# The second group's preparation moved into the first group's recurrence, q turned by VectorE from the fourth group on, and one split moved earlier

## The chip, the core and the metric

The kernel runs on one core of a Trainium2 chip. The core has a matrix engine (TensorE, PE in the profile), three engines that work on vectors (VectorE = DVE, ScalarE = ACT, GpSimd = POOL) and a queue engine (SyncE = SP) that issues transfers. Each engine takes its instructions strictly in the order of its own list, and waits on semaphores where an operand comes from elsewhere. The metric is the time of one execution on the device in microseconds (us); of several runs the median counts.

## What is computed

Three layers follow one another on 3072 tokens of width 384: a delta-rule attention, a dense layer pair, and a layer with 8 experts.

```python
# attention: B=4, H=8, S=768, D=48; q, k, v [B,H,S,D], beta [B,H,S]
k_n = k / (np.linalg.norm(k, axis=-1, keepdims=True) + 1e-06)
for t in range(S):
    kt, vt, bt = (k_n[:, :, t], v[:, :, t], beta[:, :, t, None])
    y[:, :, t] = np.einsum('bhd,bhde->bhe', q[:, :, t], state)
    v_old = np.einsum('bhde,bhd->bhe', state, kt)
    state = state + bt[:, :, :, None] * np.einsum('bhd,bhe->bhde', kt, vt - v_old)
# dense pair: x [3072,384], w_in [384,2048], w_out [2048,384]
r = np.maximum(x @ w_in, 0.0)
x = (s * (r * r) + b) @ w_out
# experts: logits = normalised x times normalised embeddings / tau; one expert for each token
h = np.maximum(x[mask] @ w1[e], 0.0)
out[mask] = gate_w[mask, None] * (h @ w2[e])
```

## The kernel before, in words

**Attention.** The 768 positions are cut into 24 chunks of 32, and 4 chunks make a group: six groups, numbered 0 to 5 here (the "second group" is group 1). A group is first prepared, then run through the recurrence, chunk by chunk.

Preparation of a group: `load_k`, `load_n` (q), `load_beta`, `load_v` issue the transfers on SP; `tr_k` and `tr_q` turn k and q on PE (16 turns each, from `kpad` and `qpad` through PSUM tiles `pp`, copied by ACT into `kqt`); `gram` forms the products k k and k q on PE (tiles `gr`), ACT copies one half (`gc`), DVE masks the other (`mt`); `lanes_1` to `lanes_3` and `scale_v` bring norms and beta in on DVE; `solve` eliminates 31 columns one after another on DVE, two instructions each (`tmp`, `T`); `lanes_out` gives `tt`.

The recurrence step of a chunk (`dstep`) is a chain between PE and DVE: `ks` (PE, tile `ch`), `X` (DVE), `tx` (PE, tile `u`), `bdu` (DVE), `ku` (PE, tile `ds`) with the new state `sst` (DVE), and `mu` (PE, into `ch`), which ACT copies into `x`. In group 0 a few idle matmuls (`warm`) stand between. The chunk s of group g is written step (g,s) below: u(1,0) is the `u` of group 1's first step, ks(2,0) the `ks` of group 2's first.

**Dense pair.** `moe1` runs 12 tiles of 256 tokens, each with 8 pairs of `mm1` and `mm2`. Tile 0 uses the weights in float32 words that have to be put together first: 16 pieces are loaded (`w_load`, in the order `W_ORDER`), scaled by ACT (`w_scale`), and joined by `x_step` (two DVE instructions and one on POOL). From tile 1 on the weights are split in two parts (`split_step`, one ACT and one DVE instruction a piece) and the matmuls run in one pass each. Two groups' worth of tiles follow each group, so the attention runs ahead of the dense pair.

**Experts.** After the last tile `ffn1` and `ffn2` run over 6 supertiles of 512 tokens. Their inputs are split by `x2_split` (ACT, then POOL) in three pieces m = 0, 1, 2.

**What sets the order.** PE, DVE, ACT and POOL run in the order in which the program is written; SP's order is made by the scheduler. `attention` keeps a list of items with due times counted in hops (a step has three: `ks`, `u`, `ds`/`mu`; group 0's first step has two) and issues those due at each quarter hop. Between quarter hops `run_moe` issues a counted number of ticks of the dense pair. Items due at 100 or later are issued after the group's last step, each followed by `PREP` ticks. In group 0's recurrence the items are the `x_step`s, one a hop. Group 1's preparation stands at 99 and later, that is behind group 0's recurrence, among tile 0's matmuls. In the groups after that each group's preparation lies within the stage of the group before it.

All PSUM tiles named `pp`, `gr`, `u`, `ds`, `xp` share one pool of three buffers.

Of the kernel before, what the change touches and what calls it, by code (L numbers as in the profile page):

```python
# [6 lines left out]
F32 = mybir.dt.float32  # L7
# [12 lines left out]
def tile_kernel(ctx, tc, q, k, v, beta, w_in, w_out, s_in, b_in, emb, tau, w1, w2, out):  # L20
# [125 lines left out]
                    in_=beta[h, 2 * r:2 * r + 2, gi * HG * C:(gi + 1) * HG * C].rearrange("g (n t) -> g n t", t=C))  # L146

    def tr_k(gi, s, eng=None):
        kqt_t[gi, s] = att.tile([128, B, 256], F32, tag="kqt", name="kqt", bufs=KQB)[0:DP]
        pp = ps_pp.tile([128, B, 128], F32, tag="pp", name="pp")  # L150
        for h in range(B):
            nc.tensor.transpose(out=pp[0:DP, h, :], in_=kpad[gi % 2][:, h, s, 0:DP], identity=ident)
        o = kqt_t[gi, s].rearrange("p h (a x t) -> p (h a) x t", a=2, x=4)[:, :, 0::3, :]
        i = pp[0:DP].rearrange("p h (a x t) -> p (h a) x t", a=2, x=2)
        if eng is nc.vector:
            nc.vector.tensor_copy(out=o, in_=i)
        else:
            nc.scalar.copy(out=o, in_=i)
# [18 lines left out]

    def tr_q(gi, h):
        tr_n(gi, h, qpad, slice(1, 3), (nc.scalar,))

    def k_rows(gi, s):
        pp = ps_pp.tile([128, B, DP], F32, tag="pp", name="kr")
# [112 lines left out]
            tt_t[gi] = att.tile([128, 2 * HG * B, C], F32, tag="tt", name="tt", bufs=2)  # L295
        nc.vector.transpose(out=tt_t[gi].rearrange("p u t -> p t u"), in_=T)

    PREP = {100: 2, 200: 5, 201: 4, 300: 2, 301: 1, 400: 5}
    st = {"hop": 0, "xs": 0, "pos": -1, "xd": {}, "gi": 0, "left": 0}

    def ks(gi, s, ch):
# [112 lines left out]
    def attention(more, first):  # L414
        for gi in range(NG):
# [4 lines left out]

            if gi == 0:
                add(0, first)
                for i in range(1, 3 * HG - 1):
                    add(i, x_step)
                add(10, x_step)
            if gi + 1 < NG:
                g2 = gi + 1
                sy = [nc.sync]
                if gi:
                    add(0, load_k, g2, sy)  # L430
                    add(0, load_n, g2, qpad, q, nc.sync)
                    add(0, load_beta, g2)
                    add(0, load_v, g2, nc.sync)
                h = 3.25
                if gi:
                    for f in (tr_k, tr_q, gram):
                        for s in range(0, HG, 2 if f is gram else 1):
                            add(h, f, g2, s)
                            h += 0.25
                else:  # L440
                    add(99, second_places)
                    for f in (tr_k, tr_q, gram):
                        for s in range(0, HG, 2 if f is gram else 1):
                            add(99 if f is tr_k and s < 2 else 100, f, 1, s)
                if gi:
                    for f, a in ((lanes_1, ()), (lanes_2, ()), (lanes_3, ()), (scale_v, (0, nc.vector)),
                                 (scale_v, (1, nc.vector))):
                        add(h, f, g2, *a)
                        h += 0.25
                    he = 11.25  # L450
                    for j in range(C - 1):
                        add(h + (he - h) * j / (C - 1), solve, g2, j)
                    add(he + 0.25, lanes_out, g2)
                else:
                    add(100, router_setup_a2)
                    add(200, lanes_1, 1)
                    add(200, lanes_2, 1)
                    add(200, lanes_3, 1)
                    add(201, scale_v, 1, 0, nc.vector)
                    add(201, scale_v, 1, 1, nc.vector)  # L460
                    add(201, router_setup_b)
                    for j in range(C - 1):
                        add(301 if j % 3 == 2 else 300, solve, 1, j)
                    add(400, lanes_out, 1)
            items.sort(key=lambda x: (min(x[0], 300) if x[0] > 100 else x[0], x[1]))

# [333 lines left out]
    with tc.manual_schedule(engines={ET.PE, ET.DVE, ET.Activation, ET.Pool}):  # L800
# [15 lines left out]
            w_load(W_ORDER[i])  # L816
        nc.sync.dma_start(out=s_sb, in_=s_in.partition_broadcast(128))
        nc.sync.dma_start(out=b_sb, in_=b_in.partition_broadcast(128))
        for i in W_ORDER[4:8]:
            w_load(i)  # L820
        for i in W_ORDER[8:]:
            w_load(i)
        router_setup_a()
        load_k(1, sy)
        gc_tile(0)
        ga = ps_a.tile([128, 2, HG * B, C], F32, tag="acc", name="gr")
        for h in range(B):
# [18 lines left out]
            tr_q(0, h)  # L846
        load_n(1, qpad, q, nc.sync)
        load_beta(1)
        load_v(1, nc.sync)
        for s in range(HG):  # L850
            k_rows(0, s)
        w_scale(11)
        for s in range(HG):
            gram_first(1, s, cg)
        for j in range(C - 1):
            solve(0, j)
            if j == 26:
                tg = ln[0][1]
                nc.tensor.matmul(out=warm_t[0][0:32, 0, 0:32], lhsT=tg[:, 25, 0:32], rhs=tg[:, 26, 0:32],
                                 start=True, stop=True)  # L860
                warm(9)
# [12 lines left out]
        def run_moe(n):  # L874
            for _ in range(n):
# [4 lines left out]
                    state["m"] = False  # L880
                    return
                state["n"] += 1
                if state["n"] % 3 == 0:
                    if cv["n"] < NU:
                        x_step()
                    elif state["n"] >= 76:
                        split_step()

        at = attention(lambda: run_moe(1), masks)
        for ticks in at:  # L890
# [264 lines left out]
        for s_ in range(NST):  # L1155
            if s_ + 2 < NST:
                x2_load(s_ + 2)
            for t in range(NTS):
# [1 line left out]
                    ffn1(s_ + 1, 2 * t)  # L1160
                    ffn1(s_ + 1, 2 * t + 1)
                ffn2(s_, t)
                if s_ + 2 < NST and t:
                    x2_split(s_ + 2, t - 1)
                if (s_, t) == (0, 0):
                    router2b()
                for _ in range(2):
# [54 lines left out]
```

## Time and profile before

| | us |
|---|---|
| runs | 917.24, 921.82, 922.56 |
| median | 921.82 |
| profiled execution, time | 918.63 |
| its span in the trace | 916.8 |
| PE busy | 839.4 (92%) |
| PE weight load busy | 770.5 (84%) |
| DVE busy | 465.3 (51%) |
| ACT busy | 458.4 (50%) |
| POOL busy | 61.9 (7%) |
| mean granted PE clock | 0.948 |

The span is the time from the first to the last instruction in the trace; the 1.8 us beyond it belong to the run's start and end. PE's busy time is modelled: its matmuls are pipelined, and a busy PE need not run at its peak. The page's chain of work that ended last holds only the last output tile, so it tells nothing of the stages that the change touches; these are read from the timeline and from windows.

### The profile page before, as it was taken

Reading aid. Unit: us, or ns where it says so; the run is one execution under the profiler, and the core shown is the slowest. Engines: PE = TensorE matmul, PEld = TensorE weight load, DVE = VectorE, ACT = ScalarE, POOL = GpSimd, SP = SyncE. Lnnn points to the kernel's source line nnn. Section 1 sums busy time; section 2 is a strip of 40 time slices with the busy share of each in tenths; the row PEclk is TensorE's granted clock in tenths of the full one; section 3 lists DMA queues with packets and bytes.
Section 4 is the critical chain, followed back from the end, with each engine's and each line's share of the span. In section 5 each row is a group of like instructions: output and inputs, shape, how many; then the busy total and the mean of one; then the engine's idle time right before and its main releaser. Section 6 shows DMA issues by size and latency. Waiting matters only on the chain. (4 is left out here: it accounts for less than half of the span.)

```text
span 916.8 us, 27694 instructions
## 1 busy us (share of the span) xinstructions
PE 839.4 (92%) x12090; PEld 770.5 (84%) x12090; DVE 465.3 (51%) x1051; ACT 458.4 (50%) x861; POOL 61.9 (7%) x71
## 2 busy tenths in 40 slices
PE   6467797876999999999999999999999999999996
PEld 4345686775989999999999999999997889889895
DVE  2979588669537942795368632225215423321101
ACT  1544646733575567565756566678653222222211
POOL 5115400000000000000000000000001011011000
PEclk7557899877999999999999999999999999999999
DMA  8683114211220222022000000015002910132000
GB/s 162 195 310 65 28 26 75 48 23 25 47 57 4 47 44 54 3 41 49 20 4 20 3 19 2 19 34 157 19 1 53 56 61 18 60 122 102 26 26 27
DMA packets 115593, 49.42 MB, mean 54 GB/s; under 512 B 89943, under 2 KB 112144, under 8 KB 115472
## 3 DMA queue, kind: packets, MB, share of 16 engines
q1 hardware_dynamic: 108560, 46.44, 22.4%
q10 hardware_dynamic: 6336, 1.18, 0.9%
q8 instruction: 95, 1.56, 0.7%
q14 instruction: 26, 0.21, 0.1%
q0 software_dynamic: 576, 0.02, 0.1%
HBM read 38.06 MB, written 9.74 MB: 52 GB/s over the span
## 5 line engine op out<-in xcount | busy, mean ns | idle before, releaser
L672 PE MATMUL acc<-gh,wp 128*128 128x256 f32 x1056 | 145.4, 284 | 0.0
L672 PEld LDWEIGHTS acc<-gh,wp 128*128 128x128 f32 x1056 | 132.6, 192 | 1.4
L635 ACT ACTIVATE r<-h 128x512 f32<-128x512 f32 x96 | 57.7, 601 | 130.5 <-PE h L627 103.4
L627 PE MATMUL h<-xh,wp 128*128 128x256 f32 x576 | 118.7, 289 | 2.4 <-ACT r L635 1.2
L627 PE MATMUL h<-xhl,wp 128*128 128x256 f32 x720 | 102.2, 287 | 0.0
L627 PEld LDWEIGHTS h<-xh,wp 128*128 128x128 f32 x576 | 94.5, 191 | 3.7 <-ACT r L635 1.6
L920 DVE SCALAR_TENSOR_TENSOR hl<-h,hh 128x512 fp32r<-128x512 f32 x46 | 31.8, 690 | 121.0 <-ACT hh L919 121.0
L649 DVE TENSOR_TENSOR gl<-r,gh 128x512 fp32r<-128x512 f32 x88 | 60.3, 685 | 62.4 <-ACT gh L647 62.4
L627 PEld LDWEIGHTS h<-xhl,wp 128*128 128x128 f32 x720 | 90.4, 189 | 1.1
L627 PE MATMUL h<-xl,wp 128*128 128x256 f32 x288 | 81.0, 281 | 0.0
L672 PE MATMUL acc<-gl,wp 128*128 128x256 f32 x528 | 76.3, 280 | 1.1 <-issue 1.1
L646 ACT ACTIVATE r<-r,b_sb,s_sb 128x512 f32<-128x512 f32 x88 | 72.0, 818 | 2.2
L377 ACT COPY x<-ch 32x384 f32<-32x384 f32 x96 | 45.2, 471 | 48.6 <-PE ch L363 47.5
L672 PEld LDWEIGHTS acc<-gl,wp 128*128 128x128 f32 x528 | 67.8, 190 | 1.3 <-issue 1.2
L289 DVE TENSOR_TENSOR T<-T,tmp 128x31 f32<-128x31 f32 (+15 forms) x186 | 65.1, 350 | 6.4
L993 POOL TENSOR_TENSOR x2l<-xr,x2h 128x512 fp32r<-128x512 f32 x15 | 19.4, 1291 | 719.4 <-DVE L L1090 592.7
L286 DVE TENSOR_TENSOR tmp<-A,T 128x31 f32<-128x31 f32 (+15 forms) x186 | 64.6, 348 | 5.0
L1003 PE MATMUL o<-w2h,hh 128*128 128x384 f32 x184 | 62.6, 340 | 0.0
L636 ACT ACTIVATE r<-r 128x512 f32<-128x512 f32 x96 | 60.7, 632 | 3.1
L1003 PE MATMUL o<-w2h,hl 128*128 128x384 f32 x184 | 62.2, 338 | 0.0
L1003 PE MATMUL o<-w2l,hh 128*128 128x384 f32 x184 | 62.1, 337 | 0.0
L1007 ACT ACTIVATE o<-o,gate 128x384 f32<-128x384 f32 x24 | 14.0, 582 | 94.1 <-PE o L1003 85.3
(215 smaller groups left out, 1437.9 us busy)
## 6 DMA issues: line engine op xcount, KB each, us to landing
wr<-in_moe_w_in SPq DMA_DIRECT2D x16, 384.0 KB
wr<-in_moe_w_out SPq DMA_DIRECT2D x8, 768.0 KB
v<-in_v SPq DMA_DIRECT2D x192, 24.0 KB
x2d<-x2s SPq DMA_DIRECT2D x24, 192.0 KB
out<-o SPq DMA_DIRECT2D x24, 192.0 KB
kpad<-in_k SPq DMA_DIRECT2D x160, 24.0 KB
qpad<-in_q SPq DMA_DIRECT2D x40, 96.0 KB
xr<-x2d SPq DMA_DIRECT2D x5, 768.0 KB
```

The lines of the kernel that those rows point to most:

```text
L286: nc.vector.tensor_tensor(out=tmp, in0=A[:, j + 1:, j:j + 1].to_broadcast([128, m, j + 1]), in1=T[:, j:j + 1, 0:j + 1].to_broadcast([128, ...
L289: nc.vector.tensor_tensor(out=T[:, j + 1:, 0:j + 1], in0=T[:, j + 1:, 0:j + 1], in1=tmp, op=ALU.subtract)
L377: nc.scalar.copy(out=x_t[gi][pb:pb + C, :, r * 96:(r + 1) * 96].rearrange("p h (g e) -> p h g e", g=2), in_=y[32 * rr:32 * rr + 32, :, :, ...
L627: nc.tensor.matmul(out=h[:, f, :], lhsT=wi_(w, 2 * j + f, m), rhs=x[:, m, :], start=(m == 0 and i == 0), stop=(m == KD - 1 and i == 2))
L635: nc.scalar.activation(out=r, in_=h, func=AF.Relu)
L636: nc.scalar.activation(out=r, in_=r, func=AF.Square)
L646: nc.scalar.activation(out=r, in_=r, func=AF.Identity, scale=s_sb, bias=b_sb)
L649: later.append((step[0] + 11, lambda: nc.vector.tensor_tensor(out=gl, in0=r, in1=gh.bitcast(F32), op=ALU.subtract)))
L672: nc.tensor.matmul(out=acc[:, m * TT:(m + 1) * TT], lhsT=wo_(w, 2 * j + f, m * 128, 128) if kk else wx_(2 * j + 1, 2 * j + f, m * 128), rh ...
L920: nc.vector.scalar_tensor_tensor(out=hl, in0=ps, scalar=0.0, in1=hh.bitcast(F32), op0=ALU.max, op1=ALU.subtract)
L993: nc.gpsimd.tensor_tensor(out=xl[:, m].rearrange("p (u t) -> p u t", u=NTS), in0=xr[:, :, m, :], in1=o.bitcast(F32), op=ALU.subtract)
L1003: nc.tensor.matmul(out=ps, lhsT=h[:, sl], rhs=w[:, f, :], start=(f == 0 and i == 0), stop=(f == KF2 - 1 and i == 2))
```

## The change

Four things are changed. (1) Group 1's k is loaded right after the first four weight pieces, its q and beta after eight, its v after twelve; its `tr_k` for chunks 0 to 2 is issued before the `warm` matmuls that stand ahead of group 0's first step, and the rest of its turns, its `gram`, its `lanes` and the first eight `solve` columns are due inside group 0's recurrence (hops 2 to 10.5). (2) Of the `x_step`s six instead of twelve lie in that recurrence; the others follow one every 8 ticks of tile 0, and the remaining `solve` columns of group 1, `scale_v` and the router's setup are spread among them, three ticks each. (3) For groups 3, 4 and 5 q is no longer turned on PE: `load_qb` loads it in 64 pieces a group instead of 8, laid out in 32 by 32 blocks, and `tr_qb` turns it by four DVE transposes a head straight into `kqt`; only three heads fit, so the fourth head's 16 pieces wait until the first head has been turned. (4) In the experts' layer the third `x2_split` piece is issued with the second, one ffn2 earlier.

```diff
@@ tr_k @@
-        kqt_t[gi, s] = att.tile([128, B, 256], F32, tag="kqt", name="kqt", bufs=KQB)[0:DP]
+        kqf_t[s] = att.tile([128, B, 256], F32, tag="kqt", name="kqt", bufs=KQB)
+        kqt_t[gi, s] = kqf_t[s][0:DP]
...
+    qn = qpad.rearrange("p h r d -> p (h r d)")[:, 0:3 * HG * 128].rearrange(
+        "p (h s r d) -> p h s r d", h=3, s=HG, r=4)
...
+    def load_qb(gi, h):
+        for g in range(2):
+            for b in range(2):
+                w = min(32, D - 32 * b)
+                for s in range(HG):
+                    t = (gi * HG + s) * C
+                    nc.sync.dma_start(
+                        out=qn[32 * (2 * g + b):32 * (2 * g + b) + 32, h % 3, s, :, 0:w],
+                        in_=q[h, g::2, t:t + C, 32 * b:32 * b + w].rearrange("r t d -> t r d"))
+
+    def tr_qb(gi, h):
+        for s in range(HG):
+            o = kqf_t[s][:, h].rearrange("p (a x t) -> p a x t", a=2, x=4)[:, :, 1:3, :]
+            nc.vector.transpose(out=o, in_=qn[:, h % 3, s].rearrange("p (a x) d -> p a x d", a=2))
...
-    PREP = {100: 2, 200: 5, 201: 4, 300: 2, 301: 1, 400: 5}
+    PREP = {300: 3, 400: 5}
@@ attention, group 0 @@
-                for i in range(1, 3 * HG - 1):
+                for i in range(1, 7):
                     add(i, x_step)
-                add(10, x_step)
@@ attention, a later group @@
-                    add(0, load_n, g2, qpad, q, nc.sync)
+                    if g2 < 3:
+                        add(0, load_n, g2, qpad, q, nc.sync)
+                    else:
+                        for x in range(3):
+                            add(0, load_qb, g2, x)
+                        add(4.25, load_qb, g2, 3)
...
-                    for f in (tr_k, tr_q, gram):
+                    if g2 > 2:
+                        h = 2.75
+                    for f in (tr_k, tr_qb if g2 > 2 else tr_q, gram):
                         for s in range(0, HG, 2 if f is gram else 1):
+                            if f is tr_qb and s == 3:
+                                h = 5
                             add(h, f, g2, s)
                             h += 0.25
@@ attention, group 1's preparation @@
-                    for f in (tr_k, tr_q, gram):
-                        for s in range(0, HG, 2 if f is gram else 1):
-                            add(99 if f is tr_k and s < 2 else 100, f, 1, s)
+                    add(2, tr_k, 1, HG - 1)
+                    for s in range(HG):
+                        add(2.5 + 0.5 * s, tr_q, 1, s)
+                    add(5, gram, 1, 0)
+                    add(5.75, gram, 1, 2)
...
-                    add(200, lanes_1, 1)
-                    add(200, lanes_2, 1)
-                    add(200, lanes_3, 1)
+                    add(7, lanes_1, 1)
+                    add(7.75, lanes_2, 1)
+                    add(8.25, lanes_3, 1)
                     for j in range(C - 1):
-                        add(301 if j % 3 == 2 else 300, solve, 1, j)
+                        if j < 8:
+                            add(8.75 + j * 0.25, solve, 1, j)
+                        else:
+                            add(300, solve, 1, j)
...
@@ start of the program @@
+        load_k(1, sy)
         for i in W_ORDER[4:8]:
             w_load(i)
-        for i in W_ORDER[8:]:
-            w_load(i)
-        router_setup_a()
-        load_k(1, sy)
...
         load_n(1, qpad, q, nc.sync)
         load_beta(1)
+        for i in W_ORDER[8:12]:
+            w_load(i)
         load_v(1, nc.sync)
+        for i in W_ORDER[12:]:
+            w_load(i)
+        router_setup_a()
...
-        w_scale(11)
+        w_scale(3)
         for s in range(HG):
             gram_first(1, s, cg)
+        for s in range(HG - 1):
+            tr_k(1, s)
+        w_scale(8)
@@ run_moe @@
-                if state["n"] % 3 == 0:
-                    if cv["n"] < NU:
+                if cv["n"] < NU:
+                    if state["n"] % 8 == 4:
                         x_step()
-                    elif state["n"] >= 76:
-                        split_step()
+                elif state["n"] % 3 == 0:
+                    split_step()
@@ experts @@
-                if s_ + 2 < NST and t:
-                    x2_split(s_ + 2, t - 1)
+                if s_ + 2 < NST:
+                    for m in ((), (0,), (1, 2), ())[t]:
+                        x2_split(s_ + 2, m)
```

Where the instructions stand is shown at three places. The names are those of the text above; a count behind a row says how often it follows itself.

First PE, at the end of group 0's preparation; the last three rows before are the start of the matmuls that stand ahead of group 0's first step. Before:

```order
L166 MATMUL pp<-ident,qpad 112x128 x16
L186 MATMUL kr<-ident,kqt 32x112 x64
L233 MATMUL gr<-kqt 32x32 x128
L859 MATMUL warm<-T 32x32
L385 LDWEIGHTS ident
L385 MATMUL warm<-ident 128x512
```

and now:

```order
L167 MATMUL pp<-ident,qpad 112x128 x16
L206 MATMUL kr<-ident,kqt 32x112 x64
L253 MATMUL gr<-kqt 32x32 x128
L153 MATMUL pp<-ident,kpad_104 112x128 x12
L899 MATMUL warm<-T 32x32
L405 LDWEIGHTS ident
L405 MATMUL warm<-ident 128x512
```

Twelve turns of group 1's k now stand ahead of the `warm` matmuls, and so ahead of group 0's first `u`.

Second PE, from `ds` to `u` around step (0,2). Before:

```order
L344 MATMUL ds<-bdu,kpad_103 48x96
L363 MATMUL ch<-bdu,mt 32x48 x32
L307 MATMUL ch<-sst,kqt 64x48 x32
L385 LDWEIGHTS ident
L385 MATMUL warm<-ident 128x512
L385 LDWEIGHTS ident
L385 MATMUL warm<-ident 128x512
L328 MATMUL u<-X,tt 32x48 x32
```

and now:

```order
L364 MATMUL ds<-bdu,kpad_103 48x96
L383 MATMUL ch<-bdu,mt 32x48 x32
L167 MATMUL pp<-ident,qpad 112x128 x4
L327 MATMUL ch<-sst,kqt 64x48 x32
L405 LDWEIGHTS ident
L405 MATMUL warm<-ident 128x512
L405 LDWEIGHTS ident
L405 MATMUL warm<-ident 128x512
L240 MATMUL gr<-kqt 32x64 x128
L348 MATMUL u<-X,tt 32x48 x32
```

A head's q turn and both of group 1's grams have come between `mu` of one step and `u` of the next.

Third DVE, from the `X` of step (0,2) to that of step (0,3). Before (rows with `wr` are `x_step`s):

```order
L313 TENSOR_TENSOR X<-v,ch 128x384 x2
L533 SCALAR_TENSOR_TENSOR wr_240<-wr_240 128x768
L535 TENSOR_SCALAR wr_240<-wr_240 128x768
L333 TENSOR_TENSOR bdu<-u,par 128x384 x2
L533 SCALAR_TENSOR_TENSOR wr_242<-wr_242 128x768
L535 TENSOR_SCALAR wr_242<-wr_242 128x768
L352 TENSOR_TENSOR sst<-ds,sst 112x4x96 x2
L533 SCALAR_TENSOR_TENSOR wr_245<-wr_245 128x768
L535 TENSOR_SCALAR wr_245<-wr_245 128x768
L313 TENSOR_TENSOR X<-v,ch 128x384 x2
```

and now, from the `sst` of step (0,2) to the same `X`:

```order
L372 TENSOR_TENSOR sst<-ds,sst 112x4x96 x2
L261 STREAM_TRANSPOSE A<-gc 128x1024
L264 MEMSET T 128x1024
L266 COPY ss<-A 128x32
L273 TENSOR_SCALAR s_1510<-s_1510 128x32
L275 RECIPROCAL nm<-s_1510 128x32
L276 TENSOR_TENSOR nm<-nm,ss 128x32
L277 TENSOR_TENSOR nm<-nm,s_1510 128x32
L278 TENSOR_SCALAR nm<-nm 128x32
L333 TENSOR_TENSOR X<-v,ch 128x384 x2
```

Where one `x_step` stood between `sst` and `X`, `lanes_1` and `lanes_2` of group 1 stand now; the `x_step`s that were there have gone among tile 0's matmuls.

## Rows read from the trace of the kernel before

**Rows 1.** Windows by stage: length, busy us of each engine, granted clock, transfers.

```profile
54.80:87.00 32.20, 25.77 (x842) 19.21 (x842) 27.88 (x44) 9.64 (x17) 13.18 (x9) 0.68 0.51 145
87.00:163.00 76.00, 59.42 (x597) 51.18 (x599) 60.07 (x125) 44.26 (x82) 12.82 (x7) 0.93 0.29 49
163.00:231.00 68.00, 54.36 (x1290) 47.94 (x1294) 49.98 (x116) 31.32 (x69) 0.00 (x0) 0.82 0.17 32
231.00:650.00 419.00, 415.10 (x7249) 401.23 (x7250) 222.37 (x503) 270.13 (x507) 0.00 (x0) 1.00 0.15 34
```

**Rows 2.** Timeline of PE: start, us, instruction; in brackets the idle time before.

```profile
50.06 4.02 PE L385 MATMUL warm<-ident 128*128 128x512 bf16 x9
54.80 1.16 PE L328 MATMUL u<-v,tt 32*32 32x48 f32 x64 [0.73 <-DVE tt L296]
...
86.12 0.88 PE L363 MATMUL ch<-bdu,mt 32*32 32x48 f32 x64
...
162.94 1.50 PE L328 MATMUL u<-X,tt 32*32 32x48 f32 x64 [6.56 <-DVE X L313]
...
230.91 1.15 PE L307 MATMUL ch<-sst,kqt 48*64 48x48 f32 x64
```

**Rows 3.** Timeline of SP: group 0's last v, weights, k of groups 1, 2.

```profile
25.89 5.96 SPq L135 DMA_DIRECT2D v<-in_v  x8
...
34.35 0.97 SPq L504 DMA_DIRECT2D wr<-in_moe_w_in  x2
...
57.82 26.35 SPq L117 DMA_DIRECT2D kpad<-in_k  x32
...
132.07 16.79 SPq L117 DMA_DIRECT2D kpad<-in_k  x32
```

**Rows 4.** Timeline, POOL's scaling of v and DVE's `solve` around it.

```profile
32.34 0.38 DVE L289 TENSOR_TENSOR T<-T,tmp 128x207 f32<-128x207 f32 x1
...
32.95 3.11 POOL L279 TENSOR_TENSOR v<-v,nmc 128x768 f32<-128x768 f32 x2 [19.49 <-DMA v<-in_v]
33.18 1.55 DVE L289 TENSOR_TENSOR T<-T,tmp 128x220 f32<-128x220 f32 x1
```

**Rows 5.** Timeline of PE: twelve turns of group 0's q, and a gram.

```profile
19.70 2.81 PE L166 MATMUL pp<-ident,qpad 128*112 128x128 f32 x12
...
110.77 1.38 PE L220 MATMUL gr<-kqt 48*32 48x64 f32 x117
```

**Rows 6.** Timeline of DVE: two `x_step`s, start and end of `lanes`, a split.

```profile
82.33 1.41 DVE L533 SCALAR_TENSOR_TENSOR wr<-wr 128x768 int32<-128x768 int32 x1
83.77 0.56 DVE L535 TENSOR_SCALAR wr<-wr 128x768 int32<-128x768 int32 x1
...
104.26 0.95 DVE L533 SCALAR_TENSOR_TENSOR wr<-wr 128x768 int32<-128x768 int32 x1
105.25 1.72 DVE L535 TENSOR_SCALAR wr<-wr 128x768 int32<-128x768 int32 x1
...
117.80 1.96 DVE L241 STREAM_TRANSPOSE A<-gc 128x1024 f32<-128x1024 f32 x1
...
124.68 0.20 DVE L276 STREAM_TRANSPOSE nmc<-nm 128x32 f32<-128x32 f32 x1
...
146.52 0.95 DVE L546 TENSOR_TENSOR wp<-wr,wp 128x768 fp32r<-128x768 f32 x1
```

**Rows 7.** Timeline of PE in group 2's stage, from `u` to group 3's gram.

```profile
256.22 0.88 PE L328 MATMUL u<-X,tt 32*32 32x48 f32 x64
...
259.99 0.60 PE L166 MATMUL pp<-ident,qpad 128*112 128x128 f32 x4
260.34 1.30 PE L672 MATMUL acc<-gh,wp 128*128 128x256 f32 x9
...
268.15 1.48 PE L220 MATMUL gr<-kqt 48*32 48x64 f32 x128
```

**Rows 8.** Waits of PE from 650 us to the end: total us, times, longest.

```profile
PE h L917 <- POOL x2l L993: 4.2, 5, 0.8
```

More of the change, by code (lines that the diff above doesn't have):

```diff
@@ L179, in tr_q @@
         tr_n(gi, h, qpad, slice(1, 3), (nc.scalar,))
+    qn = qpad.rearrange("p h r d -> p (h r d)")[:, 0:3 * HG * 128].rearrange(
+        "p (h s r d) -> p h s r d", h=3, s=HG, r=4)
+    kqf_t = {}
+    def load_qb(gi, h):
[11 more added lines that the diff above has]
+            nc.vector.transpose(out=o, in_=qn[:, h % 3, s].rearrange("p (a x) d -> p a x d", a=2))
     def k_rows(gi, s):
@@ L454, in attention @@
                 else:
-                    add(100, router_setup_a2)
-                    add(200, lanes_1, 1)
-                    add(200, lanes_2, 1)
-                    add(200, lanes_3, 1)
-                    add(201, scale_v, 1, 0, nc.vector)
-                    add(201, scale_v, 1, 1, nc.vector)
-                    add(201, router_setup_b)
-                    for j in range(C - 1):
-                        add(301 if j % 3 == 2 else 300, solve, 1, j)
+                    add(7, lanes_1, 1)
+                    add(7.75, lanes_2, 1)
+                    add(8.25, lanes_3, 1)
+                    for j in range(C - 1):
+                        if j < 8:
+                            add(8.75 + j * 0.25, solve, 1, j)
+                        else:
+                            add(300, solve, 1, j)
+                        if j in (10, 14):
+                            add(300, scale_v, 1, j // 14, nc.vector)
+                        if j == 18:
+                            add(300, router_setup_a2)
+                        if j == 24:
+                            add(300, router_setup_b)
                     add(400, lanes_out, 1)
```

## The prediction, as it was put on record

> **What bounds the kernel now.** I read the windows first, cut at the events that the change moves. From 231 to 650 us PE is busy 415 of 419 us at the full granted clock: there only less work on PE, or a new wait of PE, can change the time. Ahead of that PE has gaps and a clock between its two levels (1.2 and 2.4 GHz): granted 0.68 in group 0's recurrence (54.8 to 87 us), 0.93 in tile 0's stage (87 to 163) and 0.82 in group 1's stage (163 to 231) [rows 1]. In these three DVE is the busiest or nearly so: 27.9 of 32.2, 60.1 of 76.0 and 50.0 of 68.0 us, so it idles 4.3, 15.9 and 18.0 us [rows 1]. Then the timeline of PE gives the marks: u(0,0) at 54.80, group 0's last `mu` ends at 87.00, u(1,0) starts at 162.94 after PE stood 6.56 us waiting for DVE's `X`, ks(2,0) starts at 230.91 [rows 2].
>
> The order of instructions gives the frame of the sum. Ahead of ks(2,0) PE has 276 matmuls of the dense pair before and after the change, and from there on its list is the same but for the q turns of groups 3 to 5, until the experts. So the time changes by the shift of ks(2,0), plus the q turns, plus the moved split.
>
> **Part a, group 0's start.** Twelve turns of group 1's k now stand on PE ahead of `warm` and u(0,0), in an engine that keeps its order; behind them wait all of group 0's steps, and on ACT, where their three copies stand ahead of five pieces' scaling, the `x_step`s' operands. They need all 32 k loads. SP can start these at 34.35, where the fifth weight piece went before [rows 3]. The 32 took 26.35 us behind twelve weight pieces and 16.79 us in a quiet stretch [rows 3]; from the end of an issue (31.85) to its user's start (32.95) 1.1 us passed [rows 3, 4]. Twelve turns cost 2.8 us at the low clock [rows 5], 1.8 at three times 0.60 [rows 7]; `warm` 4.02 and the small matmul ahead of it about 0.3 [rows 2]. Low end: 34.35 + 16.79 + 1.1 + 1.8 + 4.3 = 58.3, 3.5 us later than 54.80. High end: 34.35 + 26.35 + 1.1 + 2.8 + 4.3 = 68.9, 14 later. Only the end of the third weight piece and the fourth are in flight, so I stay near the quiet row: 18 us, u(0,0) at 60, **+5**.
>
> The Trainium skill, "DMA: Bandwidth & Descriptors", section on the anatomy of one DMA, gives a fixed cost of about 2.0 us for a transfer on the GpSimd path; by it, as an estimate, the landing would add 0.9 us here and in part e each time. The row's 1.1 is used.
>
> **Part b, group 0's recurrence.** Into this chain come, on PE, four turns of k and sixteen of q, and both grams; on DVE the masks, `lanes` and five `solve` columns, in place of five `x_step`s. The first eight turns run beside `X`, the next twelve stand between `u` and `ks` of step (0,1), where PE runs without a gap: at 0.15 to 0.23 us a turn some 3.5 us in all [rows 5, 7]. The grams stand between ks(0,2) and u(0,2): two of 1.4 to 1.9 us (rows 5 has 117 of 128 matmuls in 1.38), with ACT's and DVE's reads of the first between them because the pool has three buffers; less the `X` that they run beside, +4. `lanes` take 6.9 us from 117.80 to 124.68, in place of two `x_step`s of 2.0 (1.41 + 0.56) [rows 6], +2.9, and with a `solve` column +3.5. Sum **+11**, from 7 (high clock all through) to 15 (low clock). The last `mu` ends at 87 + 5 + 11 = 103.
>
> **Part c, tile 0's stage to u(1,0).** It was 75.9 us long, DVE busy 60.1 [rows 1]. `lanes` (6.9), five `solve` columns (3, ten instructions below 0.38 [rows 4]) and three splits (0.95 each [rows 6]) leave it; three `x_step`s more come, nine for six. In this stretch one cost 0.95 + 1.72 = 2.7 us [rows 6]. So 60.1 - 6.9 - 3.0 - 2.9 + 8.0 = 55 us of DVE work. With PE and the other engines holding it up for 5 us the stage is 60 us long, **-16**; the ends are 1 and 13 us of idling, -20 to -8. PE's part, 84 ticks, is shorter than that. What is late next is DVE: the nine `x_step`s and 22 `solve` columns now share it. u(1,0) comes at 163, where it was.
>
> While POOL worked on v, a `solve` instruction took 1.55 us in place of 0.38 [rows 4]: POOL's third of an `x_step` does the same to the columns that now surround it. The Trainium skill, "GPSIMD Engine Reference", key points, says that GpSimd shares its SBUF interfaces with VectorE and contends with its instructions of two SBUF inputs, which these are; the row agrees, and the rule speaks against this mixing. Without it an `x_step` would cost DVE 1.5 us (0.95 + 0.56) and the stage would be 10 us shorter; the sum goes by 2.7.
>
> **Part d, group 1's stage.** 68.0 us, PE busy 54.4, DVE 50.0 [rows 1]. By the order PE has 28 matmuls more of the dense pair between u(1,0) and ks(2,0), but about 20 fewer up to its third step, where the chain waits for PE, and the rest among `solve` columns, where PE waits for DVE. DVE has three splits more. **-1**, from -4 to +5.
>
> **Part e, q by DVE in groups 3 to 5.** PE loses 48 turns; four delay the next matmul by 260.34 - 259.99 = 0.35 us [rows 7], so 12 x 0.35 = 4.2 us of saturated PE. ACT's 48 copies go too, and 48 DVE transposes come: 16 a group, each between the 0.20 us of a 32-column one and an eighth of the 1.96 of the 1024-column one (0.25) [rows 6] or both together, some 0.4; DVE has room (222 of 419 us [rows 1]). SP issues 64 pieces for 8, at 0.52 us 33 us a group, among prefetches. The cover is thin for the fourth head: its 16 loads start when the first head has been turned, behind `X`, that is about 2.5 us after the `u` of step (g,1). They need 16 x 0.52, the 1.1 of landing, two turns (0.8) and a store's two issues that stand among them on SP (1.0, at the same 0.52): 11.2 us, so the gram's operands are there at +13.7. PE came to the gram 268.15 - 256.22 = 11.9 us after that `u` [rows 7], without the turns 10.5. A wait of 3.2 a group gives +5.4 in all; none, at a shorter issue, -4.2. I take 1.8 a group, between the two: **+1**. Waiting DVE also holds `gl` and the masks behind it.
>
> **Part f, the split.** PE waited 4.2 us in five places, at most 0.8 each, for the third piece [rows 8]. Four of the five get one ffn2 of room: **-3.4**, to 0 if the piece behind is late instead. The first is untouched.
>
> **Sum.** +5 + 11 - 16 - 1 + 1 - 3.4 = -3.4; against the profiled execution's 918.6 that is 915. The median of the runs is 3 us higher; 916 stands for both.
>
> **Rival 1, the gaps close.** The change spreads preparation over three stages whose DVE idles 38 us together [rows 1]. If the loads come at the low end (+3.5), the recurrence grows by 9, DVE hardly idles in tile 0's stage (-20), group 1's stage gains 4, and the fourth head is in time (-4.2) and the split gives its 3.4: 900, as a median about 902. For it: the idle is there. Against: the chain of `ks`, `X`, `u`, `bdu` leaves gaps wherever it runs, and it now runs with more between its links.
>
> **Rival 2, the fourth head is late.** 4.5 us of PE a group: 13.5 - 4.2 = +9 in part e, 923. For it: the count above comes near. Against: SP's issues may be shorter than 0.52.
>
> **Rival 3, slower: group 0 waits for k.** The loads run at the slow row's rate, u(0,0) at 69 (+14), and DVE, bound in tile 0's stage, gives back 9 and not 16: +14 + 11 - 9 - 1 + 1 - 3.4 = +12.6, 931, as a median 934. It decides from about 0.75 us a load. For it: group 0's own v loads between weight pieces took 0.75 each [rows 3]. Against: those pieces have landed by then.
>
> **How the numbers follow.** Forecast 0.50, rival 1 0.22, rival 2 0.13, rival 3 0.15. The forecast's own range is 908 to 926. One per cent, about what a measurement here can tell from no change, lies at 912.6 and 931.0. Faster: rival 1 and a quarter of the forecast, 0.34. Slower: two thirds of rival 3 and a little of rival 2, 0.13. Same: 0.53. From 902 to 932 half of rival 1 and rather more than half of rival 3 are left out, 2 in 10.
>
> **What would show it.** Right: u(0,0) near 60 behind a wait of PE for k; the last `mu` of group 0 near 103; DVE without gaps to u(1,0) near 163; ks(2,0) near 230; DVE waits for q transfers of 1 to 3 us in groups 3 to 5 and as much on PE ahead of the gram; one wait for `x2l` left. Wrong: ks(2,0) before 222 or after 240, or PE waiting between 231 and 650 for something that is not q.

## The result and the profile after

The changed kernel takes 908.99 us (904.75 to 910.71) where the kernel before took 920.18 in the same comparison: a ratio of 0.987 (95% interval 0.984 to 0.989), 1.3% faster. A second comparison gave 906.22 us, 0.987 again (0.985 to 0.989). 916 was forecast, with 908 to 926 as the forecast's own range: 908.99 lies just inside its fast end and 906.22 just outside, and "within 1%", the likeliest class, is not what came. The way to it was partly another one, as the two traces show at once.

The windows of the changed kernel, cut at its own marks as [rows 1] are at those of before (length, busy us of each engine, granted clock, transfers):

```profile
60.29:103.54 43.25, 29.80 (x1119) 22.02 (x1118) 31.67 (x65) 17.73 (x43) 8.79 (x6) 0.77 0.51 138
103.54:165.97 62.43, 50.65 (x266) 42.79 (x265) 54.39 (x98) 36.56 (x54) 14.64 (x9) 0.83 0.39 92
165.97:234.23 68.26, 57.07 (x1325) 49.59 (x1325) 52.82 (x119) 37.54 (x78) 0.00 (x0) 0.90 0.16 27
234.23:650.00 415.77, 412.52 (x7236) 399.28 (x7236) 232.17 (x553) 264.60 (x462) 0.00 (x0) 1.00 0.17 35
```

The timeline of PE, for [rows 2] (in brackets the idle time before a row and what ended it; "issue" there means that PE waited for nothing that the profile names; such idle time is called a pause below):

```profile
54.33 2.17 PE L153 MATMUL pp<-ident,kpad 128*112 128x128 f32 x9 [3.42 <-DMA kpad<-in_k]
...
60.29 0.88 PE L348 MATMUL u<-v,tt 32*32 32x48 f32 x64
...
75.75 0.64 PE L240 MATMUL gr<-kqt 48*32 48x64 f32 x38
76.90 1.26 PE L240 MATMUL gr<-kqt 48*32 48x64 f32 x98 [0.50 <-issue]
...
80.46 1.57 PE L240 MATMUL gr<-kqt 48*32 48x64 f32 x90 [0.97 <-issue]
81.96 1.01 PE L348 MATMUL u<-X,tt 32*32 32x48 f32 x38
86.93 0.84 PE L348 MATMUL u<-X,tt 32*32 32x48 f32 x26 [3.96 <-issue]
...
102.04 1.50 PE L383 MATMUL ch<-bdu,mt 32*32 32x48 f32 x64
...
165.97 1.50 PE L348 MATMUL u<-X,tt 32*32 32x48 f32 x64 [1.58 <-DVE X L333]
```

Group 0's recurrence has grown from 32.2 to 43.3 us, tile 0's stage shrunk from 76.0 to 62.4, group 1's stage is as long as it was (68.3 for 68.0), and ks(2,0) starts at 234.23 where it started at 230.91. The early part has given back all that it won, and 3.3 us more in this execution. In the experts one wait is left of the five in [rows 8]:

```profile
PE h L957 <- POOL x2l L1033: 0.8, 1, 0.8
```

From ks(2,0) to the end the span shrank from 685.9 (916.8 - 230.9) to 674.0 us (908.2 - 234.2). So the gain of 8.6 us of span is 11.9 behind ks(2,0) less 3.3 ahead of it. The forecast had -3.4 in all, of which only -2.4 (+1 - 3.4) lay behind. The question is why q on DVE and the moved split are worth 12 and not 2, and where the early part's gain went.

### The profile page after: what moved, and what is told of

Read it like the earlier page. It is cut to its first block, busy times and chain, and to the rows that moved or that the text cites. A ratio compares the mean times of both kernels' runs of the same rounds, so it can differ in the third digit from the quotient of the medians.

```text
span 908.2 us, 27800 instructions
## 1 busy us (share of the span) xinstructions
PE 829.5 (91%) x12042; PEld 760.5 (84%) x12042; DVE 476.3 (52%) x1099; ACT 450.0 (50%) x813; POOL 60.9 (7%) x71
## 5 line engine op out<-in xcount | busy, mean ns | idle before, releaser
L707 PE MATMUL acc<-gh,wp 128*128 128x256 f32 x1056 | 140.8, 280 | 0.0
L707 PEld LDWEIGHTS acc<-gh,wp 128*128 128x128 f32 x1056 | 129.6, 188 | 1.3
L309 DVE TENSOR_TENSOR T<-T,tmp 128x31 f32<-128x31 f32 (+15 forms) x186 | 74.2, 399 | 6.4
```

The lines of the kernel that those rows point to most:

```text
L309: nc.vector.tensor_tensor(out=T[:, j + 1:, 0:j + 1], in0=T[:, j + 1:, 0:j + 1], in1=tmp, op=ALU.subtract)
L707: nc.tensor.matmul(out=acc[:, m * TT:(m + 1) * TT], lhsT=wo_(w, 2 * j + f, m * 128, 128) if kk else wx_(2 * j + 1, 2 * j + f, m * 128), rh ...
```

## The experiments

The first four take the change apart.

**q by DVE alone.** `load_qb`, `tr_qb` and their places go into the kernel before; nothing else:

```diff
+                    if g2 < 3:
+                        add(0, load_n, g2, qpad, q, nc.sync)
+                    else:
+                        for x in range(3):
+                            add(0, load_qb, g2, x)
+                        add(4.25, load_qb, g2, 3)
...
+                    for f in (tr_k, tr_qb if g2 > 2 else tr_q, gram):
```

> The kernel before with the third part of the change alone: q of groups 3 to 5 turned by DVE. Theory A (a turn costs saturated PE the whole duration of its row, 0.60 us for four, and no wait takes its place): 12 x 0.60 = 7.2 us less, with each of the three stages from group 2 on about 2.4 us shorter. Theory B (the prediction's price, the 0.35 us from a row of four turns to the next matmul): 4.2 less. Theory C (the prediction's forecast of this part, a wait of 1.8 us a group for the fourth head): 1 more. Theory D (the gain seen after ks(2,0) needs the shifted start, that is it comes from how the stages meet and not from q): no change.

Measured: 0.993 of before (0.991 to 0.996), that is 6.2 us less (4.0 to 8.4). From the `X` of step (2,0) to that of (5,3) its trace has 339.2 us, before 346.9. Theories C and D fall. A fits the size, B lies at the edge of the interval; the doubled turns below decide between them.

**The split alone.**

```diff
-                if s_ + 2 < NST and t:
-                    x2_split(s_ + 2, t - 1)
+                if s_ + 2 < NST:
+                    for m in ((), (0,), (1, 2), ())[t]:
+                        x2_split(s_ + 2, m)
```

> The kernel before with the fourth part alone: the third split piece of the experts one ffn2 earlier. Theory A (the page's five waits are the whole of it): 3.4 us less, experts from the first to the last ffn1 matmul 190.9 to 187.5. Theory B (the changed kernel's experts were 4.8 shorter, so a wait costs more than the row of waits shows): 4.8 less, 186.1. Theory C (the 1.4 beyond the waits come from elsewhere and differ from run to run): 3.4 to 4.8 with no stable excess.

Measured: 0.994 (0.992 to 0.996), 5.6 us less (3.5 to 7.6). From the first to the last ffn1 matmul the traces have 191.2 us in the kernel before and in the four other experiments without the moved split, to 0.1 us, and 186.4 with it, in this run as in the changed kernel: B, stable. The page of waits counts 4.2 us for five waits, all but one of which went; 3.4 us of rows was worth 4.8 us of time. One such wait, as the timeline of PE has it in the run with q alone, which still has the old split:

```profile
736.98 0.40 PE L946 MATMUL h<-x2h,w1l 128*128 128x512 f32 x1
737.21 0.50 PE L946 MATMUL h<-x2h,w1h 128*128 128x512 f32 x1
738.55 0.50 PE L946 MATMUL h<-x2l,w1h 128*128 128x512 f32 x1 [0.84 <-POOL x2l L1022]
738.89 0.39 PE L946 MATMUL h<-x2h,w1l 128*128 128x512 f32 x1
739.12 0.40 PE L946 MATMUL h<-x2h,w1h 128*128 128x512 f32 x1
```

In the stream these matmuls start 0.23 us apart, though each has a length of 0.4: the next begins ahead of the modelled end of the one in front. The wait is counted from that end (737.21 + 0.50 = 737.71 to 738.55), but from start to start it is 1.34, 1.11 more than 0.23, and the matmul behind it comes 0.34 later, 0.11 more again. So one costs 1.22 and four 4.9. The Trainium skill, "Perfetto Trace Analysis", section on the profiler window per engine type, says that the end which a profile reports for TensorE is an estimate; the rows agree.

**The early part alone.** Parts (1) and (2) of the change on the kernel before, the q turns and the split left as they were.

```diff
+        load_k(1, sy)
         for i in W_ORDER[4:8]:
             w_load(i)
...
+        for s in range(HG - 1):
+            tr_k(1, s)
+        w_scale(8)
...
+                    add(5, gram, 1, 0)
+                    add(5.75, gram, 1, 2)
```

> The kernel before with the first two parts alone: group 1's loads, turns, gram and lanes moved into group 0's stage, the joins spread over tile 0. Theory A (as in the trace of the changed kernel): ks(2,0) 3.3 us later, the time 3 more. Theory B (the prediction's parts a to d): 1 less. Theory C (the 3.3 is the lot of one execution: gaps of PE that nothing explains, 4 us each, fall here or there): between, with ks(2,0) at 231 to 232.

Measured: 1.0005 (0.998 to 1.003), 0.5 us more (1.5 less to 2.4 more). ks(2,0) starts at 231.19. Over all profiles taken here it starts at 229.6 to 233.4 in seven kernels with the old start, and at 228.7 to 234.2 in the five with the new one and its joins as changed: C. The 3.3 us of the changed kernel's trace are the lot of an execution. A falls; B's 1 us lies within the interval.

**q and the split without the early part.** Both diffs above together.

> The kernel before with the third and fourth part, without the early part. If the parts add as the two traces say (7.2 and 4.8, and the early part costs 3.3): 12 us less than before, 3 less than the changed kernel, about 905. If the early part is worth the 1 us that was predicted: 1 more than the changed kernel, about 910. If q's gain needs the early part: 3.4 to 4.8 less than before, about 916.

Measured: 905.28 us against 918.53, 0.985 (0.983 to 0.988). The two add (6.2 + 5.6 = 11.8; measured 13.3 in the medians), and the early part is not needed for them. It is as fast as the changed kernel at least; the intervals overlap, so that it is faster is not shown. In this execution PE waited 2.8 us ahead of turns of k for a transfer, in the stages of groups 2 and 3; with q on DVE these turns stand two quarter hops earlier. In the other runs that wait is 0.3 us or absent.

**Turns twice.** In the kernel before, each q turn of groups 3 to 5 is made twice.

```diff
-        for r in range(4):
+        for r in (0, 1, 2, 3) * (2 if gi > 2 else 1):
             nc.tensor.transpose(out=pp[0:DP, r].rearrange("p n t -> p (n t)"), in_=t[:, h, r, 0:DP], identity=ident)
```

> The kernel before, with each of the 48 turns of q in groups 3 to 5 made twice on PE, into the same place of PSUM; the copies stay as they are. Theory A (a turn costs saturated PE its row's duration, 0.60 for four): 7.2 us more, about 2.4 in each of three stages. Theory B (the price is from row to next matmul, 0.35 for four): 4.2 more. Theory C (what the removal won was ACT's copies or the pool's buffers, not PE): no more than 1 more.

Measured: 1.0025 (1.0004 to 1.0047), 2.3 us more (0.4 to 4.3). A falls. From the starts of all PE rows between the `X` of (2,0) and that of (5,3), each counted to the next row's start: 4.4 us for the q turns in the kernel before, 9.6 here, so the doubled ones take 0.44 for four; and 2.3 us went from other rows at the same time, 1.4 from the dense pair's and 0.9 from the gram's. Of these 2.3, 1.4 are pauses: from 231 to 650 us they add to 3.4 in the kernel before and to 2.0 here (the last section tells what they are). Without them the doubling would have cost 3.7 in this comparison, beside B's 4.2. B had the price of a turn in a row nearly right; the removal is worth more than that price.

**Copies twice.**

```diff
             if engines[s % len(engines)] is nc.scalar:
-                nc.scalar.copy(out=o, in_=i)
+                for _ in range(2 if gi > 2 else 1):
+                    nc.scalar.copy(out=o, in_=i)
```

> The kernel before, with ACT's copy of each turned q in groups 3 to 5 made twice (48 copies of 0.28 us more on ACT, and each buffer of the pool held 1.1 us longer). Theory A and B (PE's own time is what the turns cost): no change, within 1 us. Theory C (ACT and the pool's buffers are part of the price): 2 us more or above.

Measured: 1.0074 (1.0049 to 1.0099), 6.8 us more. This I had not expected: ACT is busy half of the span. The waits of PE from 231 to 650 us (total us, times, longest):

```profile
PE gr L221 <- ACT kqt L172: 4.2, 3, 1.5
PE ds L345 <- ACT kqt L172: 1.1, 3, 0.5
PE gr L221 <- DVE mt L205: 0.8, 1, 0.8
PE pp L166 <- ACT kqt L172: 0.5, 3, 0.2
```

The gram waits for the last copy, 1.2 to 1.5 us a group, and `ds` for a buffer of the pool. The kernel before has none of these waits, so it didn't pay for ACT's time as such; but its cover was used up: the fourth head's copies ended at 365.26 us in group 4's preparation, while the gram ran from 364.07 to 365.85, and that gram took 1.70 us from start to next start where the version with q on DVE took 1.42.

**The fourth head's loads twice.** In the changed kernel.

```diff
                         add(4.25, load_qb, g2, 3)
+                        add(4.25, load_qb, g2, 3)
```

> The changed kernel, with the fourth head's 16 loads of q issued twice in groups 3 to 5. SP then needs 16 x 0.53 = 8.5 us more before the second copy of the last piece has landed. In the changed kernel the fourth turn came about 1 us after its loads had landed by the rows of SP (266.5 + 1.1 against 268.33; 360.5 against 361.54; 453.4 against 454.68). If that margin is real, the turn and the gram behind it come some 7 us later and PE waits about 6 us a group: about 18 us more than the changed kernel, 8 more than before. If the turn was held by its place on DVE alone and the loads had been there long since: less than 6 more than the changed kernel.

Measured: 926.47 us, 1.0075 of before (1.0046 to 1.0105), 17 to 20 us above the changed kernel. The waits of PE and DVE in the same stretch:

```profile
PE gr L240 <- DVE kqt L199: 16.9, 3, 5.8
...
DVE kqt L199 <- DMA qpad<-in_q: 22.4, 8, 7.3
```

So the second rival's chain (loads, turn, gram) is real. 8.5 us more on SP make 5.6 us of PE's wait a group: the changed kernel has some 3 us to spare there, of which DVE's turn has 1.

**The experts' first splits earlier.** On the version with q and the split.

```diff
-            if f >= KF2 - KD:
-                x2_split(1, f - KF2 + KD)
+            if KF2 - KD <= f + 1 < KF2:
+                x2_split(1, f + 1 - KF2 + KD)
```

> The kernel before with q and the split as changed, without the early part, and the three splits of the experts' second supertile one ffn1 step earlier, for the one wait of 0.8 us that is left. If such a wait costs 1.2 us (4.8 us for four, as the experts' lengths of 191.2 and 186.4 give): experts 185.2, and 1.2 less than the version without this step, 1.48% less than before made 1.6%. If the row of the wait is all: 0.8 less. If the piece is late for another reason, or the splits now hold up ACT ahead of the first supertile's hidden tiles: no change or more.

Measured: 904.38 us, 0.985 (0.982 to 0.988): nothing, beside 0.985 without it. The last wait for `x2l` is gone, but the row below stands in its place, and the experts took 187.0 us:

```profile
696.63 0.50 PE L946 MATMUL h<-x0h,w1h 128*128 128x512 f32 x1 [1.24 <-DVE hl L949]
```

The splits now stand ahead of steps that make `hl`, and by this row it is `hl` that comes late instead.

**The changed kernel again, and three variants of its early part.** The base:

> The changed kernel itself, on the chip on which the next three run, as their base. Where the early part is worth nothing (1.0005 of before by itself), it lies beside the version with q and the split alone: 1.3 to 1.5% below before.

Measured: 906.22 us, 0.987 (0.985 to 0.989); u(0,0) at 56.88, last `mu` to 101.4, u(1,0) at 163.83, ks(2,0) at 231.82.

The second gram of group 1 behind u(0,2):

```diff
-                    add(5.75, gram, 1, 2)
+                    add(6.5, gram, 1, 2)
```

> The changed kernel with group 1's second gram one place later, behind u(0,2) and the idle matmuls and ahead of the ds of that step, in place of ahead of that u. In the changed kernel u(0,2) broke after 38 of its 64 matmuls for 4 us in which PE waited for nothing that shows, right behind the two grams. Theory A (the gap belongs to a long row of small matmuls, whichever they are): with the row broken by the two wide idle matmuls the gap goes or shrinks to 1 us, the last mu of group 0 ends 3 us earlier and ks(2,0) up to 3 earlier, if DVE then has work at hand. Theory B (tile 0's stage is bound by DVE, and what PE wins ahead of it is given back there): mu 3 earlier, ks(2,0) within 1 us of the changed kernel. Theory C (the gap lies at a place in the program): it stays, behind the gram, and nothing changes.

Measured: 0.987 (0.984 to 0.990), the same. The gap has moved from the `u` into the gram:

```profile
74.02 1.79 PE L240 MATMUL gr<-kqt 48*32 48x64 f32 x128
75.74 0.65 PE L348 MATMUL u<-X,tt 32*32 32x48 f32 x38
77.80 0.52 PE L348 MATMUL u<-X,tt 32*32 32x48 f32 x26 [1.42 <-issue]
78.26 0.60 PE L405 MATMUL warm<-ident 128*128 128x512 bf16 x2
78.79 1.60 PE L240 MATMUL gr<-kqt 48*32 48x64 f32 x100
84.55 0.67 PE L240 MATMUL gr<-kqt 48*32 48x64 f32 x28 [4.15 <-issue]
```

Counted from the first gram, it stands behind 128 + 64 + 2 + 100 = 294 matmuls; in the changed kernel behind 128 + 128 + 38 = 294. Theory C: it keeps its place in PE's list, whatever operation stands there.

The third instruction of each join on DVE:

```diff
-        nc.gpsimd.tensor_tensor(out=hi, in0=hi, in1=lo, op=ALU.add)
+        nc.vector.tensor_tensor(out=hi, in0=hi, in1=lo, op=ALU.bitwise_or)
```

> The changed kernel with the third instruction of each join on DVE in place of POOL, as a bitwise or in place of the sum (so the joined weights can differ in the words where the parts overlap). It costs DVE 0.95 us each, nine of them in tile 0's stage. Theory A (beside POOL's third a solve instruction of 0.42 takes 1.55 us, so each third takes 1.15 us of DVE anyway): the stage is 1.8 us shorter, the whole within 2 us of the changed kernel. Theory B (the long solve instructions cost nothing, because DVE has idle time in the stage): the stage is up to 8.6 us longer.

Measured: 0.988 (0.986 to 0.990), 1.1 us above the base in the medians, which is within the noise; tile 0's stage 61.4 us for 62.4. Theory A. DVE and POOL in the changed kernel, and below them the same column with the third on DVE:

```profile
113.91 0.39 DVE L306 TENSOR_TENSOR tmp<-A,T 128x231 f32<-128x231 f32 x1
114.33 1.54 DVE L309 TENSOR_TENSOR T<-T,tmp 128x231 f32<-128x231 f32 x1
114.07 1.55 POOL L571 TENSOR_TENSOR wr<-wr 128x768 int32<-128x768 int32 x1 [22.23 <-DVE wr L570]
```

```profile
113.21 0.96 DVE L571 TENSOR_TENSOR wr<-wr 128x768 int32<-128x768 int32 x1
114.08 0.40 DVE L306 TENSOR_TENSOR tmp<-A,T 128x231 f32<-128x231 f32 x1
114.51 0.40 DVE L309 TENSOR_TENSOR T<-T,tmp 128x231 f32<-128x231 f32 x1
```

The instruction beside POOL's took 1.54 us, and without it 0.40: POOL's third costs DVE 1.14 us though DVE doesn't run it, as the rule of the Trainium skill ("GPSIMD Engine Reference", key points) that stands in the prediction's part c has it.

The third left out:

```diff
-        nc.gpsimd.tensor_tensor(out=hi, in0=hi, in1=lo, op=ALU.add)
```

> The changed kernel with the third instruction of each join left out (the high words of tile 0's weights stay unjoined). Theory A (DVE sets the length of tile 0's stage, and POOL's thirds hold it 9 x 1.15 us there): the stage is about 10 us shorter, the whole 8 to 11 us less than the changed kernel. Theory B (the stage is set by PE's ticks, DVE's columns only fit between): no more than 3 less.

Measured: 900.35 us, 0.981 (0.978 to 0.985), 6 us below the base in the medians; the span is 6.4 shorter (898.1 for 904.5). Tile 0's stage:

```profile
103.18:155.55 52.37, 45.60 (x267) 39.27 (x266) 44.01 (x98) 36.49 (x54) 0.00 (x0) 0.92 0.42 102
```

It is 10.0 us shorter than the base's (62.4), and DVE's busy time 10.4 less (54.4 to 44.0): Theory A for the stage. Its length follows DVE's busy time one for one; that POOL's own time is not what counts, the variant before shows, which has no thirds on POOL either, keeps DVE busy 52.8 us and gained 1.0. In the whole 6 arrive: ks(2,0) comes 8.7 us earlier (u(0,0) came 0.8 later in this execution and the recurrence took 0.9 more), and the stages behind it took 2.3 us more than the base's, of which 1.8 are pauses in the gram (3.0 us for 1.2 up to 650 us).

## Why the prediction was off, step by step

| Term | forecast | in the changed kernel's trace | by itself, in time |
|---|---|---|---|
| a, u(0,0) | +5 | +5.5 | |
| b, to the last `mu` | +11 | +11.1 | |
| c, to u(1,0) | -16 | -13.5 | |
| d, to ks(2,0) | -1 | +0.3 | a to d: +0.5 (-1.5 to +2.4) |
| e, q by DVE | +1 | -7.1 (11.9 less f) | -6.2 (-8.4 to -4.0) |
| f, the split | -3.4 | -4.8 | -5.6 (-7.6 to -3.5) |
| sum | -3.4 | -8.6 | -12.2 and -12.1, by the two ratios |

**Parts a, c and d** were right in mechanism, and nearly in size: PE's wait for k, the lengths of both stages and their order. The bounds of part a were needed: u(0,0) lay between 55.9 and 60.3 us in the seven profiles with the new start, since SP came to the k loads at 30.6 us in one and 35.1 in another. From the end of their issue (35.07 + 17.64 = 52.71 in the changed kernel) to PE's turns (54.33) 1.6 us passed, and 1.3 to 1.9 over the seven, where the sum had 1.1. The 2.0 that the prediction cites of the Trainium skill, "DMA: Bandwidth & Descriptors", section on the anatomy of one DMA, is the page's figure for transfers on the GpSimd path. These loads are issued by SP, so the figure doesn't bear on them. Of the later start little arrives, since the first `X` of group 0 is held by other things too: in the changed kernel it came 1.9 us later than before (65.89 for 63.95), in the run of the early part alone 0.4 earlier. In part c the price of a join beside the columns (2.7 us) held, DVE was busy 54.4 us of the 55 forecast, and the stage was 2.4 us longer than that plus 5.

**Part b** met its number partly by luck. In the changed kernel three pauses of PE stood in the chain of group 0's recurrence, 0.50, 0.97 and 3.96 us in the rows above; DVE's next `bdu` waited 4.67 us for that last `u`. Before there were two:

```profile
61.40 0.53 PE L363 MATMUL ch<-bdu,mt 32*32 32x48 f32 x11 [1.12 <-issue]
...
66.50 0.52 PE L328 MATMUL u<-X,tt 32*32 32x48 f32 x11 [0.62 <-issue]
```

The forecast had no such term, and by the rows the difference, 5.4 less 1.7, makes 3.7 of the 11.1 us. The turns, grams and `lanes` that it named, less what else changed, come to the other 7.4, the low end of its 7 to 15.

Why the early part is worth nothing can be read from the windows, though no run shows it by itself. From u(0,0) to ks(2,0) DVE is busy 137.9 us in [rows 1] and 138.9 after, and idles 38 us before and 35 after. Work was moved from one stage to another, in both of which DVE is at work most of the time; it was hardly moved into its gaps. The pauses moved along with the grams: from u(0,0) to ks(2,0) those of 0.5 us or more add to 7.5 us before and, with one of 1.36 in `ks` and one of 1.48 in a gram beside the three, to 8.3 after. The first rival, that the gaps close, is refuted.

**Part e** failed, and in both of its halves. First the wait: "I take 1.8 a group" was a wait of which nothing came. The timeline of DVE after, and of PE at the gram:

```profile
255.86 0.88 DVE L199 STREAM_TRANSPOSE kqt<-qpad 128x128 f32<-128x128 f32 x4
...
268.33 0.88 DVE L199 STREAM_TRANSPOSE kqt<-qpad 128x128 f32<-128x128 f32 x4
```

```profile
259.88 0.32 PE L348 MATMUL u<-X,tt 32*32 32x48 f32 x10
...
269.67 0.57 PE L240 MATMUL gr<-kqt 48*32 48x64 f32 x35
```

The prediction let the first head be turned about 2.5 us behind the `u` of the step. It was turned 4 us ahead of that `u`, behind `X`, so the fourth head's loads started 6 us earlier than reckoned, and the last turn ended at 269.21 us, 9.3 behind the `u` and not 13.7. The prediction has the place right, "behind `X`"; but that `X` stands at 250.53 us in the trace of before, 5.7 ahead of the `u` at 256.22, and its time was not looked up. The rest of that sum was near: a turn of a head, four instructions, took 0.88 us, where it has 0.8 for "two turns".

Second the price of a turn on saturated PE. 0.35 us for four, the distance to the next matmul, was right for the row itself: in the kernel before the twelve rows take 4.4 us, against 4.2 forecast. But the removal also mended what they broke. Before, turns stood between the dense pair's matmuls of `gh`, from the row at 260.34 in [rows 7] on:

```profile
260.34 1.30 PE L672 MATMUL acc<-gh,wp 128*128 128x256 f32 x9
261.47 0.60 PE L166 MATMUL pp<-ident,qpad 128*112 128x128 f32 x4
261.83 0.60 PE L672 MATMUL acc<-gh,wp 128*128 128x256 f32 x3
262.27 0.85 PE L672 MATMUL acc<-gl,wp 128*128 128x256 f32 x6
```

After, these matmuls run in one piece:

```profile
263.25 1.54 PE L707 MATMUL acc<-gh,wp 128*128 128x256 f32 x12
264.63 0.84 PE L707 MATMUL acc<-gl,wp 128*128 128x256 f32 x6
```

Twelve of them take 1.38 us here. Before, nine and three of them took 1.13 and 0.44, with 0.36 for the turns between. So this break cost 0.19 beside the turns. From `X` of (2,0) to `X` of (5,3) the sum for the run with q alone is: turns 4.4, the dense pair's matmuls 2.5 (260.0 to 257.5), the gram 1.0 (12.3 to 11.3), less 0.2 elsewhere: 7.7 of 7.7 (346.9 to 339.2). Not all of this is breaks. Waits of PE from 231 to 650 us, before and with q alone:

```profile
PE gr L220 <- issue: 2.3, 3, 1.0
PE acc L672 <- issue: 1.1, 1, 1.1
```

```profile
PE gr L240 <- issue: 2.0, 3, 0.7
```

So 1.4 of the 7.7 are pauses that came out shorter. The one of 1.1, ahead of the matmul at 275.13 us, two other runs of the old order had as well and the ones with doubled turns and copies hadn't; it ended 1.4 us after a piece of PE's own instructions had landed, which the last section takes up, and so is no part of the price of a turn. That the rest, 1.9, is breaks throughout is not shown. The third rival's mechanism, k late in group 0, was seen in small; its price was not reached.

**Part f** was right in its mechanism and mis-sized: it took the wait's rows (0.8 each) for the loss, which is 1.2 from start to start.

So the forecast was 7 to 8 us too slow in e and 1.4 to 2 in f, and otherwise within 3, part b with the help of pauses that it did not know of. That 908.99 still lies in its range is owed to the width of the range: the step that was to cost 1 us brought 6.

## What to carry to other kernels

What PE loses to a wait or a break is the distance of starts around it less the distance of starts in the undisturbed stream. The row of a wait says less (0.84 us for 1.22), and so does the step from an inserted row to the next one (0.36, with 0.19 more for the break around it). Moving preparation into an earlier stage brought nothing here, where DVE was at work in both stages; compare the sum of the busiest engine's time over both stages first, and look whether the moved work falls into its idle time. And before a wait is priced for a chain that starts behind an event, look up that event's time in the trace, not the one next to it in the program.

## What had not been expected of the hardware

PE's pauses lie at equal counts of matmuls. In the experiment with the gram apart the two lie 26 + 2 + 100 = 128 matmuls apart. In the changed kernel the `u` broke after 38 of 64, and the second gram ahead of it after 38 of 128 (0.97 us): 128 again. The one behind the 294th was 3.6 to 5.5 us long in all seven profiles with the new start; the one 128 ahead of it 0.8 to 1.4 us in six.

No row names what PE waits for there, but the transfers do. Each trace has a queue that moves the program's own instructions; from the page of the changed kernel (packets, MB, share):

```profile
q8 instruction: 95, 1.56, 0.7%
```

That is 95 pieces of 16 KB for 12042 matmuls, one for about 127 of them and their weight loads. The pauses at 76.90, 80.46 and 86.93 us end 1.3, 1.3 and 1.4 us after such a piece has landed (75.56, 79.16, 85.49). Of the 97 pauses of 0.5 us or more behind 45 us in all fourteen traces, 92 end 1.2 to 1.7 us after one; the other five are one place, a matmul of tile 0 on the joined weights. Pieces lie 9 to 10 us apart on average, so chance would give fewer than 10 in 97. By these times PE waits for its next instructions. Most of the pauses stand in rows of small matmuls (11 ns apart in a gram), which use up a piece in a few us. During the long pause the DMA engines were full (362 GB/s from 81.96 to 86.93 us); whether that is why it is longer than the others no run shows.

DVE turns of 128 x 128 f32 in blocks of 32 took 0.22 us each in a row (four in 0.88), nearly twice the 0.11 of a turn that was doubled on PE, and were still the better choice, because DVE had idle time there and PE none. The Trainium skill, "VectorE: DVE Perf Modes", section on rules for kernel authors, advises TensorE for a 128 x 128 transpose whose result may lie in PSUM. The rows agree as to the time of one, though DVE's instruction turns only the blocks here and the load has laid these out; the 6.2 us show that beside a saturated PE the free engine was the better one.
